# Joining GpSimd loads by two pairs, first pair on SP and ScalarE, weights sooner, tokens permuted up to the store, in a two-stage attention and mixing kernel

## The chip, the cores and the metric

The kernel runs on one core of one Trainium2 chip. The metric is the device time of one execution in microseconds (us), as the median of several runs. A profile is one further execution; its span, from the first to the last instruction, is about 2 us shorter than the time. A run more than 1.5% above the fastest of its kernel counts as slow and is left out of the ratios; medians are of all runs. In the profiles PE is TensorE, PEld its weight loads, DVE VectorE, ACT ScalarE, POOL GpSimd and SP SyncE; the granted clock is the share of PE's full speed that the profile records.

## The reference, cut to what matters

```python
# stage 1: decayed linear attention; batch 4, 8 heads, 768 tokens in 12 blocks of 64, head size 64
intra = (q_block @ k_block.T * Dmask) @ v_block        # lam ** (i - j) for i >= j
inter = (q_block * lam_pow) @ kv_state
out_block = intra + inter
kv_state = lam**64 * kv_state + (k_block * rev_pow).T @ v_block
# stage 2: x = attention output as (4, 768, 512)
W_tok = (x @ w_q) @ (x @ w_k).T / 8
result = relu(W_tok @ x) @ w_out                       # f32, 4 x 768 x 512
```

A sum over tokens does not depend on their order, so stage 2 may work on permuted tokens as long as the rows are put right at the end.

## The kernel before: the parts concerned

Two heads of one batch are a pair; there are 16. Each pair needs q, k and v, which are f32 in memory. GpSimd issues their loads and has them cast to bf16 on the way. GpSimd also multiplies v by its decay (`vn`), for which the v must have landed. PE (TensorE) transposes q and k (`turn`), makes the states from k and vn, the scores from q and k, then the attention output, which is transposed (`flip`) and mixed; `po` is the last product, with the output weights, and `osb` its copy, from which SP stores the result. `warm` matmuls work on zeros and only keep PE busy. The output weights `wo` are loaded by GpSimd too.

```python
def load_q(n):
    t = stage.tile([128, 2, 3, 2 * D], BF16, tag="fq", name="fq")
    nc.gpsimd.dma_start(out=t, in_=q_rows(n))
# ... load_kv(n) the same for k and v; load(n) is both

# ... start: q of pair 0 by GpSimd, k by SP, v by ScalarE; 20 warm matmuls on PE

for n in range(NP):                       # pairs 0 to 3
    scale_v(n + 2, nc.gpsimd)             # vn(n+2): waits for v of pair n+2
    load(n + AHEAD)                       # AHEAD = 4: issues q, k, v of pair n+4
    scores(n)
    # ... flip, states(n), turn(n + 1), inter(n), values(n)

for n in range(NP, N):                    # pairs 4 to 15
    if n + 2 < N:
        scale_v(n + 2, nc.gpsimd)
    if n + AHEAD < N:
        load(n + AHEAD)
    if n == NP:
        load_wo()                         # output weights, behind pair 8
    # ... scores(n), mix_po, mix_py, flip, inter(n), values(n)
        states(n + 1)                     # needs vn(n+1)
        turn(n + 2)                       # needs q and k of pair n+2
# ... mix_po ends in one store of 128 rows (a tile):
        nc.sync.dma_start(out=out[b, t * CH : (t + 1) * CH, :], in_=osb)
```

GpSimd works through its list in order: while `scale_v` waits, no load is issued.

## Time and profile before

| | before |
|---|---|
| time, median of runs | 110.88 us (110.18 to 111.33) |
| span of the profile | 108.6 us |
| PE busy | 93.9 us, 87% |
| GpSimd busy | 67.3 us, 62% |
| GpSimd waiting for v | 11.2 us |
| PE waiting for `wo` | 3.2 us, once |
| vn of pair 14 done | 79.4 us |
| k transposes of pair 14 | 78.70 us |
| states of pair 14 on PE | 82.07 us |
| last group of 24 po matmuls starts | 99.22 us |

The last rows come from the timeline. They are marks. The lines of the profile are in the prediction below.

### The profile page before, as it was taken

What the parts mean: (1) busy time and instruction counts of PE and PEld (TensorE: products, weight loads), DVE (VectorE), ACT (ScalarE), POOL (GpSimd) and SP (SyncE); (2) the same over time, 40 slices, a digit from 0 to 9 for tenths busy, and PEclk for the clock granted to TensorE, in tenths of its full rate; (3) what the DMA queues carried; (4) which work ended last, traced back from release to release, by engine and by line L of the source; (5) the groups of instructions that cost most, each with busy time, mean ns of one, the idle gap of its engine ahead of it and who ended that gap; (6) DMA issues with size and microseconds to landing.
All of it is one profiled execution on the core that took longest, in us unless ns stands there. A gap on an engine that the chain in (4) does not pass through costs nothing. (4 is left out here: it accounts for less than half of the span.)

```text
span 108.6 us, 3486 instructions
## 1 busy us (share of the span) xinstructions
PE 93.9 (87%) x1492; PEld 59.2 (55%) x1492; DVE 66.5 (61%) x162; ACT 65.1 (60%) x118; POOL 67.3 (62%) x69
## 2 busy tenths in 40 slices
PE   5998998887979878089999999999999999999950
PEld 2335565655765664034777758475867646643410
DVE  2115997882898595500787897739697892426330
ACT  4314977687337577423747498875468887439430
POOL 5999719999999999945996499729523100000000
PEclk9999999999999999966999999999999999999999
DMA  0999999999999999999999999999993024424382
GB/s 8 227 190 162 163 171 144 165 136 152 132 140 141 135 141 126 177 161 163 309 160 228 193 91 138 201 164 307 174 213 33 0 103 178 150 90 162 149 322 109
DMA packets 67406, 17.12 MB, mean 158 GB/s; under 512 B 63808, under 2 KB 64320, under 8 KB 67392
## 3 DMA queue, kind: packets, MB, share of 16 engines
q0 software_dynamic: 59632, 9.57, 119.5%
q1 hardware_dynamic: 6208, 6.95, 19.0%
q10 hardware_dynamic: 1552, 0.39, 1.6%
q8 instruction: 11, 0.18, 0.6%
q14 instruction: 3, 0.02, 0.1%
HBM read 20.19 MB, written 6.29 MB: 244 GB/s over the span
## 5 line engine op out<-in xcount | busy, mean ns | idle before, releaser
L284 DVE TENSOR_TENSOR pr<-sc,maskc 128x384 bf16<-128x384 f32 x64 | 31.1, 549 | 4.3 <-PE sc L272 3.8
L195 POOL TENSOR_TENSOR vn<-fv,DvI 128x768 bf16<-128x768 bf16 x14 | 20.8, 1484 | 16.2 <-DMA fv<-in_v_dram 11.2
L435 PE MATMUL po<-wo,rmT 128*128 128x512 bf16 x96 | 24.3, 401 | 3.4 <-DMA wo<-in_moe_w_out_dram 3.2
L324 ACT CAST xT<-oa 128x384 bf16<-128x384 f32 x32 | 16.8, 598 | 4.6 <-PE oa L316 4.6
L449 ACT COPY osb<-po 128x512 f32<-128x512 f32 x21 | 12.3, 585 | 11.7 <-PE po L435 10.8
L229 ACT COPY kT<-trk 128x768 bf16<-128x768 bf16 x16 | 12.8, 802 | 9.8 <-PE trk L225 9.3
L435 PEld LDWEIGHTS <-rmT 128*128 128x128 bf16 x96 | 9.2, 102 | 15.4 <-DMA wo<-in_moe_w_out_dram 3.3
L79 POOL DMA_DIRECT2D fv<-in_v_dram x15 | 15.5, 1035 | 0.0
L79 POOL DMA_DIRECT2D fk<-in_k_dram x15 | 15.5, 1032 | 0.0
L73 POOL DMA_DIRECT2D fq<-in_q_dram x16 | 14.3, 891 | 0.8 <-POOLq L567 0.8
L341 DVE COPY xnat<-xp 128x768 bf16<-128x768 bf16 x12 | 6.7, 555 | 12.7 <-PE xp L336 12.5
L428 ACT ACTIVATE rmT<-pm 128x384 bf16<-128x384 f32 x28 | 11.6, 518 | 0.0
L272 PE MATMUL sc<-qT,kT 64*128 64x128 bf16 x192 | 10.1, 217 | 1.2 <-ACT kT L229 0.3
L456 PE MATMUL warm<-blank 128*128 128x512 bf16 x28 | 9.0, 485 | 1.3 <-DVE blank L100 1.3
L336 PE MATMUL xp<-ident,xT 128*128 128x128 bf16 x96 | 8.7, 220 | 1.3 <-ACT xT L324 0.6
L216 DVE TENSOR_TENSOR qT<-trq,dq 128x768 bf16<-128x768 bf16 x16 | 8.8, 548 | 1.0 <-PE trq L210 1.0
L336 PEld LDWEIGHTS <-xT 128*128 128x128 bf16 x96 | 6.4, 98 | 5.4 <-ACT xT L324 2.6
L272 PEld LDWEIGHTS <-kT 64*128 64x128 bf16 x192 | 6.4, 94 | 5.0 <-issue 2.9
L295 PE MATMUL oa<-qT,gs 64*64 64x128 bf16 x160 | 8.1, 222 | 1.0 <-DVE gs L253 0.9
L225 PE MATMUL trk<-ident,fk 128*64 128x128 bf16 x180 | 7.6, 220 | 1.1 <-DMA fk<-in_k_dram 1.1
L210 PE MATMUL trq<-ident,fq 128*64 128x128 bf16 x192 | 8.2, 220 | 0.4 <-DMA fq<-in_q_dram 0.4
L316 PE MATMUL oa<-pr,vn 128*64 128x128 bf16 x192 | 8.3, 222 | 0.0
(55 smaller groups left out, 106.3 us busy)
## 6 DMA issues: line engine op xcount, KB each, us to landing
out_dram<-osb SPq DMA_DIRECT2D x24, 256.0 KB, 2.1
fq<-in_q_dram POOLq DMA_DIRECT2D x16, 192.0 KB, 5.8
fk<-in_k_dram POOLq DMA_DIRECT2D x15, 192.0 KB, 6.3
fv<-in_v_dram POOLq DMA_DIRECT2D x15, 192.0 KB, 7.2
wo<-in_moe_w_out_dram POOLq DMA_DIRECT2D x1, 512.0 KB, 8.8
v<-in_v_dram ACTq DMA_DIRECT2D x1, 384.0 KB, 5.3
k<-in_k_dram SPq DMA_DIRECT2D x1, 384.0 KB, 6.4
wqk_f<-in_moe_w_q_dram SPq DMA_DIRECT2D x1, 128.0 KB, 3.4
```

Source lines behind the costliest of these rows:

```text
L73: nc.gpsimd.dma_start(out=t, in_=q_rows(n))
L79: nc.gpsimd.dma_start(out=t, in_=kv_rows(n, src))
L195: eng.tensor_tensor(out=vn, in0=fv, in1=DvI[:, 2 * kk : 2 * kk + 2, :].unsqueeze(3).to_broadcast([128, 2, NCH, D]), op=ALU.mult,)
L229: nc.scalar.copy(out=kT, in_=trk)
L272: nc.tensor.matmul(sc[a, hl][:, cc, :], kT[r, c * CH : (c + 1) * CH], qchunk(n, r, c), start=True, stop=True, skip_group_check=True,)
L284: nc.vector.tensor_tensor(out=t, in0=sc[a, hl], in1=maskc, op=ALU.mult)
L324: nc.scalar.copy(out=xT[b][:, kk, a * HALF : (a + 1) * HALF].rearrange("d (c p r) -> d c r p", c=3, r=2), in_=oa[a].rearrange("d c (r p) - ...
L336: nc.tensor.transpose(xp[:, t, :], xT[b][:, kk, t * CH : (t + 1) * CH], ident)
L428: nc.scalar.activation(out=to, in_=pms[dd, n], func=ACT.Relu, scale=1.0 / 8.0)
L435: nc.tensor.matmul(po, M[b]["rmT"][:, kt, t * CH : (t + 1) * CH], wo[:, kt, :], start=(kt == 0), stop=(kt == 3),)
L449: nc.scalar.copy(out=osb, in_=po)
L456: nc.tensor.matmul(w, blank[:, 0:128], blank, start=True, stop=True)
```

## The change

Its intent: less time spent issuing on GpSimd (one DMA for two pairs), no wait for the output weights, an earlier first pair, and a dense copy on ScalarE in place of one that reorders tokens; the order is then put right by storing each 128-row tile as two halves.

```diff
-WARM = 20
+WARM = 8
...
-    stage = ctx.enter_context(tc.tile_pool(name="stage", bufs=9))
+    stage = ctx.enter_context(tc.tile_pool(name="stage", bufs=5))
...
+    def load(n, count=1):            # count=2: one DMA each for q, k, v of two pairs
+        hs = slice(2 * kk, 2 * kk + 2 * count)
+        fq = stage.tile([128, 2 * count, 3, 2 * D], BF16, tag="fq" + tag, name="fq")
...
-    load_q(0)
+    q0 = consts.tile([128, 2, 3, 2 * D], F32, name="q0")
+    nc.sync.dma_start(out=q0, in_=q_rows(0))      # then k0; v0 by ScalarE as before
...
-            nc.scalar.copy(out=xT[...].rearrange("d (c p r) -> d c r p", c=3, r=2), in_=...)
+            nc.scalar.copy(out=xT[b][:, kk, a * HALF : (a + 1) * HALF], in_=oa[a])
...
-        nc.sync.dma_start(out=out[b, t * CH : (t + 1) * CH, :], in_=osb)
+        rows = out[b, t * CH : (t + 1) * CH, :].rearrange("(p r) d -> r p d", r=2)
+        for r in range(2):
+            nc.sync.dma_start(out=rows[r], in_=osb[r * 64 : r * 64 + 64, :])
...
     for n in range(NP):
         scale_v(n + 2, nc.gpsimd)
-        load(n + AHEAD)
+        if n + 4 < 6:
+            load(n + 4)
+        elif n % 2 == 0:
+            load(n + 4, 2)
+            load_wo()
...
             scale_v(n + 2, nc.gpsimd)
-        if n + AHEAD < N:
-            load(n + AHEAD)
-        if n == NP:
-            load_wo()
+        if n % 2 == 0 and n + AHEAD < N:
+            load(n + AHEAD, 2)
```

More of the change, by code (lines that the diff above doesn't have):

```diff
@@ L69, in kv_rows @@
         return src[b, 2 * kk : 2 * kk + 2].rearrange("h (c p) d -> p h c d", p=128)
-    def load_q(n):
-        t = stage.tile([128, 2, 3, 2 * D], BF16, tag="fq", name="fq")
-        nc.gpsimd.dma_start(out=t, in_=q_rows(n))
-        staged[n, "q"] = t
-    def load_kv(n):
-        for nm, src in (("k", k), ("v", v)):
-            t = stage.tile([128, 2, NCH, D], BF16, tag="f" + nm, name="f" + nm)
-            nc.gpsimd.dma_start(out=t, in_=kv_rows(n, src))
-            staged[n, nm] = t
-    def load(n):
-        load_q(n)
-        load_kv(n)
-    load_q(0)
+    def load(n, count=1):
+        b, kk = pairs[n]
+        hs = slice(2 * kk, 2 * kk + 2 * count)
+        tag = str(count)
+        fq = stage.tile([128, 2 * count, 3, 2 * D], BF16, tag="fq" + tag, name="fq")
+        nc.gpsimd.dma_start(
+            out=fq, in_=q[b, hs].rearrange("h (a p r) d -> p h a (r d)", p=128, r=2)
+        )
+        kv = []
+        for nm, src in (("k", k), ("v", v)):
+            t = stage.tile([128, 2 * count, NCH, D], BF16, tag="f" + nm + tag, name="f" + nm)
+            nc.gpsimd.dma_start(
+                out=t, in_=src[b, hs].rearrange("h (c p) d -> p h c d", p=128)
+            )
+            kv.append(t)
+        for i in range(count):
+            staged[n + i] = [t[:, 2 * i : 2 * i + 2] for t in (fq, *kv)]
+    lam_all = consts.tile([128, H], F32, name="lam_all")
+    nc.sync.dma_start(out=lam_all, in_=lam.partition_broadcast(128))
+    q0 = consts.tile([128, 2, 3, 2 * D], F32, name="q0")
+    nc.sync.dma_start(out=q0, in_=q_rows(0))
+    k0 = consts.tile([128, 2, NCH, D], F32, name="k0")
+    nc.sync.dma_start(out=k0, in_=kv_rows(0, k))
     v0 = consts.tile([128, 2, NCH, D], F32, name="v0")
     nc.scalar.dma_start(out=v0, in_=kv_rows(0, v))
-    staged[0, "v"] = v0
-    lam_all = consts.tile([128, H], F32, name="lam_all")
-    nc.sync.dma_start(out=lam_all, in_=lam.partition_broadcast(128))
-    k0 = consts.tile([128, 2, NCH, D], F32, name="k0")
-    nc.sync.dma_start(out=k0, in_=kv_rows(0, k))
     wqk_f = consts.tile([128, 2, 4, DHY], F32, name="wqk_f")
@@ L140 @@
     load(2)
+    load(3)
     lnl = consts.tile([128, H], F32, name="lnl")
@@ L181, with take @@
     xT, xnat = {}, {}
-    def take_k(n):
+    def take(n):
         if n == 0:
-            kn = nat.tile([128, 2, NCH, D], BF16, tag="kn", name="kn")
+            fq = nat.tile([128, 2, 3, 2 * D], BF16, tag="q0", name="q0b")
+            nc.vector.tensor_copy(out=fq, in_=q0)
+            kn = nat.tile([128, 2, NCH, D], BF16, tag="k0", name="k0b")
             nc.vector.tensor_copy(out=kn, in_=k0)
-        else:
-            kn = staged.pop((n, "k"))
-        L[n]["kn"] = kn
+            staged[0] = [fq, kn, v0]
+        L[n].update(zip(("fq", "kn", "fv"), staged.pop(n)))
     def scale_v(n, eng):
@@ L193, in scale_v @@
         vn = nat.tile([128, 2, NCH, D], BF16, tag="vn", name="vn")
-        fv = staged.pop((n, "v"))
+        fv = L[n]["fv"]
         eng.tensor_tensor(
@@ L204, in turn @@
         b, kk = pairs[n]
-        fq, kn = staged.pop((n, "q")), L[n]["kn"]
+        fq, kn = L[n]["fq"], L[n]["kn"]
         trq = pst([128, 3, 2, CH], BF16, "trq")
@@ L323, in values @@
                     )
-            nc.scalar.copy(
-                out=xT[b][:, kk, a * HALF : (a + 1) * HALF].rearrange(
-                    "d (c p r) -> d c r p", c=3, r=2
-                ),
-                in_=oa[a].rearrange("d c (r p) -> d c r p", r=2),
-            )
+            nc.scalar.copy(out=xT[b][:, kk, a * HALF : (a + 1) * HALF], in_=oa[a])
         del L[n]
@@ L458 @@
     warm(WARM)
+    take(0)
     make_dq(0)
-    take_k(0)
     turn(0)
     scale_v(0, nc.vector)
-    warm(4)
+    warm(6)
     make_dq(1)
-    load(3)
+    take(1)
     for n in range(NP):
+        take(n + 2)
         scale_v(n + 2, nc.gpsimd)
-        load(n + AHEAD)
+        if n + 4 < 6:
[3 more added lines that the diff above has]
+            load_wo()
         scores(n)
@@ L483 @@
             cast_wqk()
-        take_k(n + 1)
         turn(n + 1)
@@ L493 @@
         if n + 2 < N:
+            take(n + 2)
             scale_v(n + 2, nc.gpsimd)
-        if n + AHEAD < N:
-            load(n + AHEAD)
-        if n == NP:
-            load_wo()
-        for d in (1, 2):
-            if n + d < N and "kn" not in L[n + d]:
-                take_k(n + d)
+        if n % 2 == 0 and n + AHEAD < N:
+            load(n + AHEAD, 2)
         if n == NP:
```

## The prediction

> **What bounds the kernel now.** I read the page's busy shares first, then the stretches of 4 us, then the waits, then GpSimd's own timeline.
>
> ```profile
> PE 93.9 (87%) x1492; PEld 59.2 (55%) x1492; DVE 66.5 (61%) x162; ACT 65.1 (60%) x118; POOL 67.3 (62%) x69
> ```
>
> PE leads, but an average over stages hides a stop in the middle. The stretches show it (columns: window, busy us and instructions of PE, weight loads, DVE, ACT and GpSimd, then granted clock, DMA share, GB/s):
>
> ```profile
> 8.00:12.00 4.00, 3.56 (x53) 1.86 (x54) 2.90 (x6) 2.47 (x4) 4.00 (x5) 1.00 2.24 164
> 12.00:16.00 4.00, 3.55 (x92) 2.63 (x88) 4.00 (x10) 3.05 (x5) 0.83 (x2) 1.00 2.25 163
> ...
> 36.00:40.00 4.00, 2.95 (x66) 2.15 (x59) 2.91 (x8) 3.17 (x7) 4.00 (x5) 1.00 1.87 134
> 40.00:44.00 4.00, 2.87 (x62) 1.85 (x61) 2.76 (x9) 2.69 (x7) 4.00 (x5) 1.00 1.33 134
> 44.00:48.00 4.00, 1.37 (x5) 0.60 (x6) 0.97 (x3) 0.61 (x2) 3.25 (x4) 0.90 2.02 171
> 48.00:52.00 4.00, 4.00 (x35) 1.87 (x34) 0.55 (x1) 1.75 (x3) 1.86 (x2) 0.67 2.23 173
> ```
>
> From 44 to 48 us PE is nearly empty, and after it runs at a granted clock of 0.67. The waits name the cause, and name GpSimd's own longest wait too:
>
> ```profile
> POOL vn L195 <- DMA fv<-in_v_dram: 11.2, 5, 3.8
> ...
> PE po L435 <- DMA wo<-in_moe_w_out_dram: 3.2, 1, 3.2
> ```
>
> The output weights `wo` are issued by GpSimd at 37.81 and wanted at 43.5; they land 8.8 us after issue, at 46.6. The twelve po matmuls behind them then take 4.45 us instead of three times the 0.87 us of a later po group, so the stop costs 3.2 + about 1.8 = 5 us. Ahead of it, GpSimd paces everything:
>
> ```profile
> 29.19 1.51 POOL L195 TENSOR_TENSOR vn<-fv,DvI 128x768 bf16<-128x768 bf16 x1
> 30.61 0.89 POOL L73 DMA_DIRECT2D fq<-in_q_dram  x1
> 31.48 1.03 POOL L79 DMA_DIRECT2D fk<-in_k_dram  x1
> 32.49 1.04 POOL L79 DMA_DIRECT2D fv<-in_v_dram  x1
> 33.51 1.51 POOL L195 TENSOR_TENSOR vn<-fv,DvI 128x768 bf16<-128x768 bf16 x1
> ```
>
> One turn is vn (1.5) plus three issues (2.9), 4.3 to 4.4 us a pair, back to back from 17 to 47 us, while PE's first pairs follow each other at 3.78 us. PE waits only briefly for it (fk 1.1 us, vn 0.6 us in all). Late in the kernel the loads are no longer issue-bound; they share the DMA engines with the stores. The transfer times, first of 26 to 37 us, then of 62 to 76 us (last number: us from issue to landing):
>
> ```profile
> fq<-in_q_dram POOLq DMA_DIRECT2D x3, 192.0 KB, 4.1
> fk<-in_k_dram POOLq DMA_DIRECT2D x3, 192.0 KB, 4.7
> fv<-in_v_dram POOLq DMA_DIRECT2D x3, 192.0 KB, 4.9
> ```
> ```profile
> out_dram<-osb SPq DMA_DIRECT2D x5, 256.0 KB, 5.5
> fq<-in_q_dram POOLq DMA_DIRECT2D x3, 192.0 KB, 5.0
> fk<-in_k_dram POOLq DMA_DIRECT2D x3, 192.0 KB, 6.2
> fv<-in_v_dram POOLq DMA_DIRECT2D x3, 192.0 KB, 7.8
> ```
>
> The first two of the 4 us rows give the ceiling of these loads: 163 to 164 GB/s while nothing but queued loads ran. A pair is 3 x 192 KiB = 590 KB, so 3.6 us of the DMA engines whoever issues it; a store of 256 KB took about 0.7 us of them when alone.
>
> **What the Trainium skill says.** "DMA: Bandwidth & Descriptors", section "Issuing engines are not separate DMA queues": transfers started by SP, ScalarE and GpSimd run on the same 16 DMA engines and interleave, and another issuer saves only issue time. The trace agrees: fv takes 7.8 us beside stores, 4.9 without. The same page, "Rules for kernel authors": coalesce small transfers, and two transfers to disjoint partition halves serialize and gain nothing. The first is the change's idea, the second touches its split stores; no run here has either yet. "TensorE: Matmul & The Clock Gate", "Part 1: The HAM clock gate": an idle window of about 3.4 us brings the half clock back. The trace agrees: 3.15 us of wait, then the 0.67 above.
>
> **The change part by part.**
> Output weights: issued behind pairs 6 and 7, near 29 to 30 us instead of 37.8. Even at 9 us to landing that is 39, before the first use at 43. Worth up to 5 us at that place.
> First pair: q of pair 0 leaves GpSimd (1.01 us of issue) and comes as 384 KB of f32 on SP, ahead of k. It adds a DVE cast like k's (0.60 us). Before, q landed at 8.58 and k at 7.68; now q should land near 6.4, but k, behind it, near 8.4. Scores of pair 0 start from k: cast 0.6, transposes 0.5, copy 0.8, so 10.4, against 10.39 before. Eight warm matmuls at 0.43 end at 4.7 instead of 8.2, so the clock may be half around 8 to 12 us. I take 0 to +2 us here, hidden by later waits for data.
> Pairs of loads: issue of a double load costs, from 0.89 for 768 runs and 1.03 for 1536, about 1.05 + 1.3 + 1.3 = 3.7 instead of 5.9 us. GpSimd drops from 67.3 to about 56 us busy (five doubles save 2.2 each).
> Order of tokens: the xT copy writes densely; a dense copy of the same size (wqT) took 478 ns, xT 598, so 32 x 0.12 = 3.8 us off ScalarE, which is 60% busy: nearly nothing on the path. Stores become 48 of 128 KB; SP issues one in 0.33 us, so the last store ends about 0.3 us later.
>
> **The step that decides: who may issue when.** On GpSimd the order is vn(n+2), then load(n+4), and vn waits for its v to land. With single loads another pair is still in flight at that moment. With doubles nothing is: load(8,9) is issued only after v(6,7) has landed and vn(6) is done. So the doubles form a chain. One link, as an estimate from the trace: 1.4 us from issue to first packet, 2 x 3.6 = 7.2 us of transfer, 0.4 to landing, 1.5 for vn: 10.5 us for two pairs, plus 0.7 for each store that falls inside. Before, GpSimd needed 8.7 for two; PE in pairs 9 to 12 took 20.3 us for four, 10.1 for two. So a link with two or three stores, 12 us, is longer than what PE needs.
>
> The chain: load(6,7) starts near 25.5 (26.28 before, less what the shorter start gives). vn(6) 36.0 (before 35.0), vn(8) 46.5, vn(10) 59.8 (four stores inside, 2.8), vn(12) 72.4 (three, 2.1), vn(14) 84.2 (two, 1.3). Before, vn(14) was done at 79.4 and its user on PE, the state matmuls, ran at 82.07. So the gain at `wo` puts PE some 4 us ahead at pair 8, and it is given back as PE waits of 1 to 3 us at the states of pairs 10, 12 and 14. From those states to the end the work is as before, 108.6 - 82.07 = 26.5 us, and the end moves by 84.2 - 82.07 = 2.1, minus nothing, plus 0.3 for the last store, minus 0.2 for the copies. Span 110.8; the time was 2.2 above the span, so **113.0 us**.
>
> **Rivals.** (1) The chain is shorter than I think, because stores fall into the 3 us between links when the engines rest, or the load starts sooner. Without any store in the way it is 25.5 + 5 x 10.5 = 78 for vn(14), PE is then ahead throughout, and the end is near 104 to 107. For it: DMA share is not full after 52 us. Against it: the eleven stores of pairs 7 to 12 need 7.4 us somewhere. (2) The half clock returns after each wait near 3 us, as it did at 46.6; each could add 1 to 2 us, to 116 to 118. For it: the 0.67 row; against: waits estimated under 3 us stay below the window. (3) GpSimd was the true bound, and fewer issues release it: 4.4 to about 3.3 us a pair would give PE its 3.8 us pace to pair 7, and the result is near 105. Against: a transfer is 3.6 us a pair and can't be shortened by joining.
>
> **Range and chances.** A link uncertain by 0.6 us, five times, and 2 us for the stores give about 4 us either way at vn(14); earlier arrivals help only until PE binds. So 107.0 to 118.0 in 8 of 10. The lower side is close: faster by over 2% (under 108.6) 0.25, within 2% 0.32, slower (over 113.1) 0.43.
>
> **What would show it.** Right: no wait of po for wo; GpSimd busy under 60; its waits for fv far above 11.2 us, at pairs 6, 8, 10, 12, 14, with each double load issued right after such a vn; PE's dps matmuls waiting for vn at even pairs; fv of a double landing 7 to 9 us after its own issue. Wrong: vn never waits long, or PE's waits move to the start (half clock at 5 to 12 us), or the double's transfer is well under 7 us.

## The result, and the profile after

The changed kernel took 132.13 us (131.14 to 133.72), against 110.88 us before. The ratio is 1.189, with a 95% interval of 1.178 to 1.201. A ratio here and below is the mean time of one kernel's fast runs over that of the other's of the same rounds, so it is not quite the ratio of the medians. The predicted time was 113.0 with a range up to 118.0: the direction was right, the size far off.

The busy line of the page of the changed kernel:

```profile
PE 97.3 (75%) x1470; PEld 61.2 (47%) x1482; DVE 69.4 (53%) x163; ACT 62.4 (48%) x118; POOL 57.3 (44%) x53
```

GpSimd is 10 us less busy, as it was meant to be, and PE's share fell from 87% to 75%. Its work is nearly the same; there is more waiting. The stretches of 4 us (columns as in the prediction: window, PE, weight loads, DVE, ACT, GpSimd, granted clock, DMA share, GB/s) show where:

```profile
44.00:48.00 4.00, 0.84 (x22) 0.62 (x21) 1.47 (x5) 0.00 (x0) 1.03 (x1) 0.71 2.32 154
48.00:52.00 4.00, 3.58 (x41) 2.29 (x43) 1.16 (x3) 2.83 (x7) 0.41 (x1) 0.50 0.96 63
52.00:56.00 4.00, 3.98 (x54) 2.44 (x55) 1.35 (x3) 2.40 (x5) 4.00 (x4) 0.94 0.26 27
...
68.00:72.00 4.00, 3.51 (x67) 2.47 (x67) 1.22 (x6) 1.45 (x3) 2.61 (x3) 0.81 0.03 2
...
92.00:96.00 4.00, 0.53 (x20) 0.37 (x14) 1.15 (x4) 0.89 (x3) 0.00 (x0) 1.00 1.92 232
96.00:100.00 4.00, 3.40 (x29) 1.81 (x31) 1.95 (x4) 0.80 (x1) 0.48 (x1) 0.61 1.05 90
```

Two things alternate. PE stops while the DMA engines are full (44 to 48, 92 to 96), and then the DMA engines stop while PE works (27 GB/s from 52 to 56, 2 GB/s from 68 to 72). Before, no stretch between 4 and 84 us was under 100 GB/s. GpSimd's timeline around one such turn tells why:

```profile
39.63 1.07 POOL L76 DMA_DIRECT2D fq<-in_q_dram  x1
40.69 1.42 POOL L82 DMA_DIRECT2D fk<-in_k_dram  x1
42.10 1.42 POOL L82 DMA_DIRECT2D fv<-in_v_dram  x1
43.53 1.49 POOL L200 TENSOR_TENSOR vn<-fv,DvI 128x768 bf16<-128x768 bf16 x1
51.59 1.47 POOL L200 TENSOR_TENSOR vn<-fv,DvI 128x768 bf16<-128x768 bf16 x1 [6.56 <-DMA fv<-in_v_dram]
53.00 1.05 POOL L76 DMA_DIRECT2D fq<-in_q_dram  x1
```

The double load of pairs 8 and 9 is issued from 39.63. GpSimd does vn(7), then stands at vn(8), which needs the v just issued; it lands after 51.4. Only behind vn(8), at 53.00, comes the next double load. This is the chain that the prediction named. Its links are the distances between first issues: 26.62, 39.63, 53.00, 70.80, 84.83, and vn(14) done at 101.0, so 13.0, 13.4, 17.8, 14.0 and 16.2 us. No store ran in the first two, but the first carried the weights too (issued at 30.48), so the second is the clean one. The waits:

```profile
POOL vn L200 <- DMA fv<-in_v_dram: 43.9, 6, 11.0
...
PE trk L230 <- DMA fk<-in_k_dram: 12.1, 5, 3.8
...
PE dps L247 <- POOL vn L200: 2.8, 3, 1.6
```

GpSimd waits 43.9 us for v, against 11.2. PE's own waits are mostly not for vn but for k: the k transposes of pair n+2 stand in turn n, a turn before the states that need vn(n+2), so the late k stops PE first. No wait of PE for `wo` is left.

With the marks from above the loss adds up. The k transposes of pair 14 start at 96.38 instead of 78.70 (17.7 us later). From there to the states of pair 14, at 101.39, it is 5.0 instead of 3.4 us (1.6), with the clock at 0.61 in that stretch; but vn(14) was done only at 101.0, so at the full clock PE would have waited for it, and by this reading the low clock accounts for 0.4 us at most. From the states to the last po group 17.0 against 17.2 (-0.2). From the start of that group to the end 12.1 instead of 9.3 (2.8). The sum, 21.9 us, is the difference of the spans, 130.5 and 108.6.

### The profile page after: what moved, and what is told of

It reads as the page before. It is cut to its first block, busy times and chain, and to the rows that moved or that the text cites. A ratio compares the mean times of both kernels' runs of the same rounds, so it can differ in the third digit from the quotient of the medians.

```text
span 130.5 us, 3484 instructions
## 1 busy us (share of the span) xinstructions
PE 97.3 (75%) x1470; PEld 61.2 (47%) x1482; DVE 69.4 (53%) x163; ACT 62.4 (48%) x118; POOL 57.3 (44%) x53
## 5 line engine op out<-in xcount | busy, mean ns | idle before, releaser
L200 POOL TENSOR_TENSOR vn<-fv,DvI 128x768 bf16<-128x768 bf16 x14 | 20.7, 1482 | 44.0 <-DMA fv<-in_v_dram 43.9
L435 PE MATMUL po<-wo,rmT 128*128 128x512 bf16 x88 | 23.4, 395 | 1.0 <-issue 0.4
L230 PE MATMUL trk<-ident,fk 128*64 128x128 bf16 x180 | 8.0, 227 | 12.1 <-DMA fk<-in_k_dram 12.1
L329 ACT CAST xT<-oa 128x384 bf16<-128x384 f32 x32 | 13.8, 484 | 5.9 <-PE oa L321 5.9
L341 DVE COPY xnat<-xp 128x768 bf16<-128x768 bf16 x12 | 6.7, 557 | 12.3 <-PE xp L336 12.1
L82 POOL DMA_DIRECT2D fk<-in_k_dram x10 | 12.3, 1226 | 0.0
L82 POOL DMA_DIRECT2D fv<-in_v_dram x10 | 12.2, 1219 | 0.0
L277 PE MATMUL sc<-qT,kT 64*128 64x128 bf16 x192 | 11.1, 239 | 1.4 <-PE sc L277 0.9
L230 PEld LDWEIGHTS <-fk 128*64 128x64 bf16 x180 | 6.0, 113 | 13.0 <-DMA fk<-in_k_dram 13.0
L76 POOL DMA_DIRECT2D fq<-in_q_dram x10 | 10.0, 1001 | 0.0
L277 PEld LDWEIGHTS <-kT 64*128 64x128 bf16 x192 | 7.4, 103 | 5.6 <-issue 2.9
L247 PE MATMUL dps<-vn,fk 128*64 128x128 bf16 (+2 forms) x150 | 6.5, 216 | 3.1 <-POOL vn L200 2.8
L458 PE MATMUL warm<-blank 128*128 128x512 bf16 x17 | 7.6, 601 | 1.5 <-DVE blank L103 1.3
```

The lines of the kernel that those rows point to most:

```text
L76: nc.gpsimd.dma_start(out=fq, in_=q[b, hs].rearrange("h (a p r) d -> p h a (r d)", p=128, r=2))
L82: nc.gpsimd.dma_start(out=t, in_=src[b, hs].rearrange("h (c p) d -> p h c d", p=128))
L200: eng.tensor_tensor(out=vn, in0=fv, in1=DvI[:, 2 * kk : 2 * kk + 2, :].unsqueeze(3).to_broadcast([128, 2, NCH, D]), op=ALU.mult,)
L230: nc.tensor.transpose(trk[hl * 64 : hl * 64 + 64, c * CH : (c + 1) * CH], kn[:, hl, c, :], ident)
L277: nc.tensor.matmul(sc[a, hl][:, cc, :], kT[r, c * CH : (c + 1) * CH], qchunk(n, r, c), start=True, stop=True, skip_group_check=True,)
L329: nc.scalar.copy(out=xT[b][:, kk, a * HALF : (a + 1) * HALF], in_=oa[a])
```

## The experiments

Before is run again with each set; its medians lay between 110.8 and 111.4 us. Most sets have three rounds, `e9` five, `e10` and `e11` one. The set of `e5` to `e8` had a wider spread of before (109.1 to 113.2), so their verdicts at 2% are unclear by the interval (as are those of `e11` and `e12`), though `e5`'s lies above 1.02 throughout. All results were correct.

**Does the order of issue make the loss?** In `e1_loads_first` only the order on GpSimd changes: each load stands ahead of the vn of its turn. No race arises, since every double has a buffer of its own.

```diff
-        take(n + 2)
-        scale_v(n + 2, nc.gpsimd)
         if n + 4 < 6: load(n + 4)
         elif n % 2 == 0: load(n + 4, 2); load_wo()
+        take(n + 2)
+        scale_v(n + 2, nc.gpsimd)
 ... the same two swapped in the second loop
```

> The changed kernel with one edit: on GpSimd each load is issued ahead of the vn multiply of the same turn, not behind it. Doubles, first pair, token order, stores all stay. Chain theory (a double load can only be issued when the double before it has landed, so nothing is in flight meanwhile): the links of 13.4 to 17.8 us disappear, vn of pair 14 is done near 76 to 80 us instead of 101, time 110 to 116 us (2.8 us of it the split stores at the end). Rival (double loads are slow in themselves, or the half clock at the start and the stores make the loss): time stays above 125.

Measured: 111.96 us, ratio 1.006 (0.999 to 1.013). Three runs lay between 111.4 and 112.1. The profiled execution of that set took 208.5 us, slow from start to end, and is left out (the last section returns to it), so the same kernel was run again for a profile:

> The changed kernel with loads ahead of vn once more, for a profile of the fast state (the one taken had [...]208 us, where three timed runs gave 111.4 to 112.1). Expected 112 us, vn of pair 14 done by 80 us against 101.

112.02 us. GpSimd's timeline in this run:

```profile
39.90 1.05 POOL L76 DMA_DIRECT2D fq<-in_q_dram  x1
40.95 1.42 POOL L82 DMA_DIRECT2D fk<-in_k_dram  x1
42.36 1.41 POOL L82 DMA_DIRECT2D fv<-in_v_dram  x1
46.77 2.90 POOL L200 TENSOR_TENSOR vn<-fv,DvI 128x768 bf16<-128x768 bf16 x2 [3.00 <-DMA fv<-in_v_dram]
49.62 1.06 POOL L76 DMA_DIRECT2D fq<-in_q_dram  x1
```

Here the load at 39.90 is that of pairs 10 and 11, and the vn it stands ahead of, at 46.77, are those of pairs 8 and 9. Doubles start 7.6 to 9.7 us apart instead of 13 to 18, and GpSimd waits 12.0 us for v. vn of pair 14 is done at 75.2 us instead of 101. So 20 of the 21 us hang on two calls that changed places. The rival, that doubles are slow in themselves, falls as the cause of this loss.

**Are singles, in the old order, free of it?** `e2_single_loads` is the changed kernel with single loads behind each vn.

```diff
-        if n + 4 < 6:
-            load(n + 4)
-        elif n % 2 == 0:
-            load(n + 4, 2)
+        load(n + 4)
+        if n == 2:
             load_wo()
 ... and load(n + AHEAD) on every turn of the second loop; 9 stage buffers
```

> The changed kernel with single loads throughout, each behind the vn of its turn as in the kernel before, weights still issued behind pair 6. Chain theory: 109 to 114 us, because another pair is always in flight while vn waits; GpSimd waits for v some 10 to 15 us in all, not 44. Rival (first pair, half clock, token order or stores make the loss): above 125.

Measured 115.69 us, ratio 1.038 (1.029 to 1.048); GpSimd waits 16.6 us for v (in a profiled run of 118.4 us). The bulk of the loss is gone, as the chain theory says, though the time lies 1.7 us above the expected range. The other parts of the change cost more than I had set aside; the next runs show what.

**The joined loads in the kernel before.** `e4_before_doubles_wo` gives the kernel before the doubles from pair 6 and the weights behind the first of them, and nothing else (but for the buffers that the doubles need).

```diff
         scale_v(n + 2, nc.gpsimd)
-        load(n + AHEAD)
+        if n + 4 < 6: load(n + 4)
+        elif n % 2 == 0: load(n + 4, 2); load_wo()
 ... second loop: on even n, load(n + AHEAD, 2); no load_wo()
```

> The kernel before with the double loads from pair 6 on and the output weights behind the first of them, nothing else. Chain theory: 126 to 130 us, nearly the whole loss with the old first pair and the old stores. Rival (first pair and stores matter more): 112 to 118.

Measured 129.34 us, ratio 1.161 (1.150 to 1.172). Doubles and weights together make nearly the whole loss, with the old first pair and old stores; the weights alone make little of it (`e7` below).

**The stores.** `e3_whole_stores` takes the token order and the half stores out of the changed kernel; `e5_split_stores` puts them alone into the kernel before.

```diff
 e3 against the changed kernel (e5 is the same with signs exchanged, on the kernel before)
-            nc.scalar.copy(out=xT[b][:, kk, a * HALF : (a + 1) * HALF], in_=oa[a])
+            nc.scalar.copy(out=xT[...].rearrange("d (c p r) -> d c r p", ...), in_=oa[a].rearrange(...))
-        for r in range(2):
-            nc.sync.dma_start(out=rows[r], in_=osb[r * 64 : r * 64 + 64, :])
+        nc.sync.dma_start(out=out[b, t * CH : (t + 1) * CH, :], in_=osb)
```

> The changed kernel with the tokens put in order at the ScalarE copy again and one whole store per tile. If the split stores cost only what the tail shows (SP issues of 0.54 to 0.60 us each, the last matmuls waiting for osb), 129 to 130 us, 2.5 to 3 less. Rival (split stores also slow the loads in the middle, where ten of them lie inside one 17.8 us link): 122 to 126.

> The kernel before with the token order and the two half stores per tile, nothing else. If only the tail pays (SP issues of 0.54 and 0.60 us for the halves of a tile against 0.33 for a whole one, so 1.2 us a tile where PE needs 0.87): 113 to 114.5 us. Rival (dense ScalarE copies pay for it): 110 to 111.

`e3` took 129.35 us, 2.8 less than the changed kernel. vn of pair 10 starts at 69.3 and 69.4 us in the two, so the halves do not slow the loads in the middle. `e5` took 114.73 us, ratio 1.048 (1.028 to 1.068): 3.9 us by the medians. It reaches its last po group at 100.31 and needs 12.2 us from there, like the changed kernel and unlike the 9.3 before. In the end of the changed kernel's timeline the copies to `osb` now wait for a buffer that a store still reads:

```profile
123.11 0.59 ACT L449 COPY osb<-po 128x512 f32<-128x512 f32 x1 [1.30 <-DMA out_dram<-osb]
124.50 0.42 DVE L444 COPY osb<-po 128x256 f32<-128x256 f32 x1 [1.70 <-DMA out_dram<-osb]
```

SP takes 0.47 to 0.60 us to issue a half where a whole store took it 0.33. Its line at the end:

```profile
120.11 7.51 SPq L452 DMA_DIRECT2D out_dram<-osb  x12
```

The twelve halves of the last six tiles keep SP busy for 7.5 us without a break, 1.25 a tile, while PE makes the six in 5.35, 0.89 each. So SP is the bound from 120.1 us on.

**The first pair.** `e6_first_pair` is the kernel before with pair 0 by SP and ScalarE in f32, 8 warm matmuls first and 6 after; `e12_first_pair_warm` is the same with 20 first. In both, the load of pair 3 also moves up, to just behind that of pair 2, as in the changed kernel.

```diff
-WARM = 20                    (e12 keeps 20)
+WARM = 8
-    load_q(0)
+    nc.sync.dma_start(out=q0, in_=q_rows(0))      # f32, ahead of k0
+            nc.vector.tensor_copy(out=fq, in_=q0)
-    warm(4)
+    warm(6)
 ... load(3) behind load(2); take_k(0) ahead of make_dq(0)
```

> The kernel before with pair 0 by SP and ScalarE in f32, 8 warm matmuls, then 6. If the half clock from 8 to 15 us in the changed kernel's profile and the first scores at 13.3 instead of 10.4 us last to the end: 112.5 to 114. Rival (hidden behind the loads, which pace the first pairs anyway): 110.5 to 111.5.

> The kernel before with pair 0 by SP and ScalarE in f32 and six warm matmuls after the first turn as before (112.15 us), but 20 warm matmuls at the start instead of 8. If the half clock at 8 to 13 us made the loss of 1.3 us or 2.4%: 110.3 to 111. Rival (later k and the extra cast make it): 111.8 to 112.5.

112.15 us (ratio 1.024, 1.014 to 1.033) and 112.61 us (ratio 1.016, 1.009 to 1.023). The two do not differ clearly. In `e6` PE ran its first transposes at half pace and its scores of pair 0 began at 12.89 us; in `e12` it ran at full pace and they began at 11.49, against 10.39 before. This earlier start bought nothing that the runs can tell, so the slow transposes are not shown to cost anything at the end. In the changed kernel vn of pair 2 starts at 16.55 us, before at 15.97, although its v was issued at 8.00 and not 8.93. That the larger f32 transfers of pair 0 hold up all loads behind them fits with this, but no run isolates it.

**The weights.** `e7_wo_sooner` only moves them in the kernel before.

```diff
         load(n + AHEAD)
+        if n == 2:
+            load_wo()
 ... and no load_wo() behind pair 8
```

> The kernel before with the output weights issued behind pair 6 (near 30 us) instead of behind pair 8. The stop of 3.2 us on PE and the half clock after it go: 106 to 108 us if nothing takes their place. Rival (a wait for vn or fk takes the place of the wait for the weights, as loads stay where they were): 109.5 to 111.

111.73 us, ratio 1.019 (1.004 to 1.034): no gain, as the rival said (0.7 us above its range). The wait for `wo` is gone, and this line of PE's timeline stands in its place:

```profile
40.66 0.85 PE L210 MATMUL trq<-ident,fq 128*64 128x128 bf16 x12 [3.30 <-DMA fq<-in_q_dram]
```

PE waits 3.30 us for q of pair 7, which now lies behind the weights and lands at 40.6, and goes on at half pace. The transfer moved forward on a full queue pushed back the loads that it overtook.

**The disputed cost by itself.** Even the clean link was 13.4 us, not 10.5. Which part of it is longer? `e10_chain_of_singles` makes a chain of single loads, one in flight.

```diff
-AHEAD = 4
+AHEAD = 3
-    load(3)                      # ahead of the loops
```

> The disputed cost by itself: the kernel before with the load distance cut from 4 pairs to 3, so that a single load is issued only when the one before it has landed and its vn is done. A link is then a fixed part plus one pair's transfer, where the double's is the fixed part plus two. As predicted (fixed 3.3, a pair 3.6): 6.9 us a link without stores. As the doubles' links now suggest (13.3 for two, with the bytes moving for about 7.6 of it): fixed 5.5 to 6, so 9 to 9.7 us a link, and a time of 150 to 165 us.

162.33 us in time. The seven links without stores were 8.0 to 9.3 us, 8.6 on average (two of them with the weights alongside), so less than the 9 to 9.7 that I expected by then, and more than the 6.9 of the prediction. The DMA view of one such link, from 34.7 to 43.6 us in 40 slices of 0.22 us, shows the shape of a load that runs alone:

```profile
GB/s 0 0 0 0 0 74 0 14 38 93 72 98 171 184 169 161 151 144 155 154 145 129 138 149 158 143 94 51 18 10 10 3 0 0 0 0 0 0 0 0
...
fq<-in_q_dram POOLq DMA_DIRECT2D x1, 192.0 KB, 4.1
fk<-in_k_dram POOLq DMA_DIRECT2D x1, 192.0 KB, 5.1
fv<-in_v_dram POOLq DMA_DIRECT2D x1, 192.0 KB, 5.4
```

About 1.6 us pass from the first issue to the first bytes, 4.5 until all but some 2% of them have moved, 1.2 from there to the landing of v (issued at 36.64, landed 5.4 later), and 1.6 for vn up to the next issue: 8.9 us. The same view for the double of pairs 8 and 9, 39.6 to 53.0 in slices of 0.33 us (the first two slices still belong to the weights):

```profile
GB/s 21 9 0 0 0 15 64 109 107 115 179 183 183 177 141 139 150 156 156 158 154 152 153 157 159 159 158 158 194 58 21 3 9 2 0 0 0 0 0 0
...
fv<-in_v_dram POOLq DMA_DIRECT2D x1, 384.0 KB, 9.3
```

Its v was issued at 42.10 and landed 9.3 us later. The four parts are 1.7, 8.0, 2.1 and 1.6 us, 13.4 in all, where the prediction had 1.4, 7.2, 0.4 and 1.5. So alone, the transfer is 0.8 to 0.9 us longer than the queue's 164 GB/s would have it, with five slow slices at the start of the double (15 to 115 GB/s) and 139 to 194 after them; and from the last bytes to the landing it takes 0.8 to 1.7 us more than predicted. In the kernel before, whose loads overlap, no slice from 26 to 37 us fell under 74 GB/s. The difference of the two chains, 13.4 - 8.6 = 4.8 us for the second pair, is no rate: it holds all of these parts, and the double's issues, which are 1.0 us longer. Why the double's landing takes longer than the single's is not shown.

**A version that beats both.** If order is what counts, the kernel before can gain from it too. `e8_doubles_first` is `e4` with loads ahead of vn. `e9_singles_first` is the kernel before with only the two calls exchanged in both loops; the weights stay behind pair 8.

```diff
 e9, both loops
+        load(n + AHEAD)
         scale_v(n + 2, nc.gpsimd)
-        load(n + AHEAD)
```

> The kernel before with doubles from pair 6, weights behind the first of them, and every load issued ahead of the vn of its turn; old first pair, old stores. By the first run of this order (112.0 with first pair and split stores changed too) less what those cost: 105 to 108 us, faster than both. Rival (joining gives nothing once the order is right): 109 to 111.

> The kernel before with each single load issued ahead of the vn of its turn, nothing else; the weights stay behind pair 8, but that point comes near 34 us instead of 37.8, with pairs up to 8 already queued ahead of them. Theory (order of issue against a wait is what matters, and the weights must lie behind the pairs that are used before them): 105 to 107.5 us, under both kernels. Rival (the weights' 3 us of transfer always takes the place of some pair's): 109 to 111.

`e8` took 109.03 us (ratio 0.996, 0.982 to 1.011): 20 us better than `e4` by order alone, but not clearly better than before. It misses the range that I gave, 105 to 108. PE waits there for k of a double twice, 3.8 us in all. `e9` took 106.79 us (ratio 0.954, 0.949 to 0.960; its fast runs 105.6 to 106.4) and beats both kernels. Its profiled run was one of its slower ones, with a half clock from 27.5 to 34.4 us, yet none of PE's longer waits is for a DMA any more:

```profile
PE xp L336 <- ACT xT L324: 2.6, 1, 2.6
PE warm L456 <- DVE blank L100: 1.3, 1, 1.3
PE oa L295 <- DVE gs L253: 1.2, 4, 0.3
```

The weights are issued at 33.7 instead of 37.8 us, with pairs up to 8 already ahead of them, and are there when PE comes to them. The loads move 160 to 185 GB/s in every slice of the page from 8 to 50 us.

## Why the prediction was wrong

**The chain: right.** The step "who may issue when" named the mechanism. `e1` and `e11` undo it and nothing else, and win 20 us back; `e4` makes it in the kernel before, with the weights moved too, and loses 18.

**The size of a link: the step that failed.** The prediction put a link at "1.4 us from issue to first packet, 2 x 3.6 = 7.2 us of transfer, 0.4 to landing, 1.5 for vn". The clean link, from 39.63 to 53.00, took 13.4 us and not 10.5: 1.7 to the first bytes, 8.0 of transfer, 2.1 to landing, 1.6 for vn. So the term most off is the landing, 2.1 us against 0.4; the transfer was 0.8 too short, the rest 0.4. The 3.6 us a pair came from a stretch in which nine loads were queued, while in a chain, by its own definition, nothing is queued; what the 0.4 rests on, the prediction does not say. (v of a double landed 9.0 to 13.8 us after its own issue, where 7 to 9 was expected.) The five links came to 74.4 us, against 58.7 predicted: 14.0 us of the difference is this size and 1.7 the stores. With 1.1 us for a later start of the chain (26.62, not 25.5) and 2.9 after vn(14), that is all of the 19.7 us by which the span was missed. The view of 26 to 37 us in the prediction was nearer, though loads overlap there: v landed 4.9 us after its own issue, so 6.8 after the first of its three, and with vn 8.3, where `e10` showed 8.6. With 3.6 for the second pair that makes 11.9 for a double, still 1.5 short.

**Stores in the links: right in size, low in number.** I took 0.7 us for each, and nine of them (four, three, two). In the three links with stores SP issued five, one and five whole tiles, and they were 4.4, 0.7 and 2.8 us longer than the clean one: 0.7 a tile on average, with the two links of five unlike each other.

**Who waits for the chain: partly wrong.** I expected PE to stop at the states for vn. It stopped mostly one step sooner, at the transposes for k, 12.1 us against 2.8. Both hang on the same double load, and in the last link vn(14) at 101.0 came just ahead of its states at 101.39.

**The rival of the half clock: it came, smaller than the main loss.** I held waits under 3 us to be too short for it. Four of the five waits for k were 2.3 to 3.9 us long, and the clock fell in four later stretches. From 46 to 52 us it stood at 0.50, during and after the wait of 2.3 us that ended at 48.2, with one of 1.6 us just before. That the trace agreed with a window of 3.4 us was a loose reading from the start, since the wait in the kernel before was 3.15. As the marks show, vn(14) bounds what the last of these falls cost at 0.4 us.

**The weights: wrong as a gain of their own.** "Worth up to 5 us at that place" holds for the place only. `e7` shows the same 3.3 us as a wait for q of pair 7.

**The last store: wrong.** I gave it 0.3 us for one more issue. `e3` and `e5` put it at 2.8 to 3.9: two halves take SP 1.25 us a tile where one whole took 0.33, and in the last six tiles they set the pace. The Trainium skill's page "DMA: Bandwidth & Descriptors", section "Rules for kernel authors", says not to bother with disjoint partition halves, since they serialize. The runs agree that nothing is gained, and show that something is lost.

**The first pair: right in time, the reason open.** 0 to 2 us was expected and 1.3 measured (`e6`). Full pace and first scores 1.4 us sooner did not reduce it (`e12`); the cause stays open.

**The dense copy: right.** 484 ns each instead of 598. No gain of it is seen in the time, and no run has it alone.

## What to carry to other kernels

When an in-order engine both issues loads and waits for loads, write each issue ahead of the wait, and count how many loads are in flight at the moment of the wait: joining two loads into one can take that count from one to zero. Never use a queue's throughput as the duration of a transfer that will run alone; take it from issue to landing, of a transfer with nothing ahead of it. And when a transfer is brought forward on a queue that is already full, look at what it overtakes: here the wait only moved (`e7`).

## What the Trainium skill lacked or had wrong

- "DMA: Bandwidth & Descriptors", "Anatomy of one DMA": its fit for a GpSimd DMA, about 2.0 us + bytes / 436e3, gives 2.5 us for a load of 192 KB. A q load at the head of an empty queue, with k issued behind it, took 4.1 us from issue to landing (`e10`). Its runs in memory are 512 bytes of f32, cast on the way. The page gives no figure for such a load.
- The same page, "Rules for kernel authors": small transfers should be coalesced into large ones. Here joining loads of 192 KB to 384 KB lost 18 us where each is issued behind a wait (`e4`, weights moved too), and gave 109.0 against 106.8 us for singles where none is (`e8`, `e9`, which also differ in the place of the weights). The rule lacks the condition that another load stays in flight. The row on overlap in the same table, to issue early and wait late, comes near it without the link to joining.
- The same page, "Issuing engines are not separate DMA queues": issue time is called usually small beside the DMA. For half stores on SP it was 0.47 to 0.60 us each against 0.33 for a whole one, and it set the pace of the last six tiles (7.5 us of issues in the changed kernel; `e5` lost 3.9 us).
- "TensorE: Matmul & The Clock Gate", "Part 1: The HAM clock gate": it tells of a clock stuck at a quarter for over 50 us. One execution of `e1` was slow from start to end, 208.5 us, but not by that ratio: the last 24 po matmuls took 14.3 us instead of 5.35, so 2.7 times as long, and no change of the granted clock was recorded, though the page warns that these records are unreliable. The next execution took 111.9 us. The page has no state of this ratio; its cause stays open.
